# A written-out order searched anew, warm-up products in one run, and a last output tile stored in two halves

## The chip, the cores and the metric

The kernel runs on one core of one Trainium2 chip. A core has a matrix engine (TensorE, PE in the profile; its weight loads are listed apart as PEld), VectorE (DVE), ScalarE (ACT), GpSimd (POOL) and SyncE (SP), each with its own stream of instructions. POOL and SP issue DMA transfers. The metric is the device time of one execution in microseconds; the kernel before took 204.93 us (median of five runs, 204.13 to 205.15).

## The reference

Sparse attention is followed by a gated feed-forward block. With 4 batches, 8 heads, 768 positions, and heads of 64:

```python
k_chunks = k.reshape(B, H, nc, chunk, D)              # 24 chunks of 32 keys
ub = sum(maximum(q * k_min, q * k_max), axis=-1)      # a bound for each query and chunk
top_chunks = argsort(where(causal, ub, -1e9))[..., -6:]
attn = softmax(where(selected and causal, q @ k.T / 8, -1e9))
x = (attn @ v), heads side by side                    # [4, 768, 512]

h = maximum(x @ w_in, 0); u, v = h[..., :512], h[..., 512:]
v_n = (v - mean(v)) / sqrt(var(v) + 1e-6)
v_s = einsum('ts,bsd->btd', w_spatial, v_n) + b_spatial
out = (u * v_s) @ w_out                               # [4, 768, 512] float32
```

## The kernel before

Two heads of one batch make a pair; there are 16 pairs, four to a batch. A pair is worked on in steps, and each step is a small function with a name. The digits that follow a name are the pair and, after it, the head of the pair or a part; for the feed-forward steps they are the batch and the tile of 128 positions (0 to 5).

Attention steps of pair i:

- `lk`, `lq`, `lv`: loads of k, q and v, issued on POOL (for two pairs at once, except the first). `win`, `wsp`, `wout` and `lb` load the feed-forward weights there too.
- `kT`, `qT`: six and five transposes of 128x128 on TensorE. `kmax`, `kmin` (`k_bound`, L686) reduce the transposed keys over chunks on DVE, `kb` (L708) packs them, `rq` (L731, L733) takes the positive and negative part of q. `ub` is the product of both, the bound.
- `top` (L752) takes the eight largest bounds of each query, and `sel` (L778) writes the selection beside q. `aT` transposes q with its selection on TensorE, and `ac` (L800) copies that to SBUF on ACT or DVE. From pair 8 on, `aTd` (L803) does both as one DMA transpose from SP.
- `kh` (L574) sets up four pairs of score operands at the start from the constant `expand`; `kop` (L715, L717) copies the transposed keys into them. For pairs 0 and 1 ACT does it, for pairs 2 to 7 DVE, and from pair 8 on it is a DMA on SP, behind a copy `kc` (L703) of the keys from PSUM to SBUF.
- `sc` (L810) are the scores, six groups for a head, each in one of three PSUM banks; the selection is part of the product, since unselected chunks get a large negative term. `ex` (L819) is the exponential on ACT. `tri` (L825) clears the upper triangle on POOL, for batches 1 to 3.
- `av` (L836) is the product with v in three parts; there is one PSUM bank for it. `rc` and `nm` (L841, L846) divide by the sum on DVE. `x` brings the result into place, transposed: by TensorE and a DVE copy (`xp`, then L864) for pairs 0 to 3 and 15, by a DMA transpose from SP (L855) for the others.

Feed-forward steps of batch b, tile ti: `v` and `u` (products with `w_in`), `va` and `ua` (ACT), `bs` and `vs` (statistics on DVE), `rs` (ACT), `vn` (DVE), `s` (product with the transposed `w_spatial`), `gt` (L973, the gate on DVE, into one of three buffers), `gd` (L988, a DMA transpose of the gate from SP that frees this buffer), `o` (product with `w_out`), `oc` (L993, the copy from PSUM) and `os` (L997, the store on SP). The last two tiles take `gp`, transposes on TensorE, in place of the DMA. All feed-forward products have the line L930. They need all four pairs of their batch, so those of batch 0 start after `x3`, and those of a batch lie among the attention steps of the next.

The order of all this is not left to a scheduler. `ORDER` is one string with the names of all steps, and the kernel runs the functions in that order. Each engine's stream is the string with the other engines' steps left out, and each engine works strictly through its own. So a step that waits holds all steps behind it on its engine. The string was made by a planner in the same file (`Sim`, `build`): it has a cost for each step, limits on buffers, priorities by due time, and a list `flip` of steps that change between ACT and DVE. Of this, only the string, the engine of each step and a few sizes reach the chip.

At the start TensorE has 65 products of a zero tile, `dm0` to `dm64`, placed one by one among the first steps (L873). Nothing reads them.

Of the kernel before, what the change touches and what calls it, by code (L numbers as in the profile page):

```python
# [11 lines left out]
F32 = mybir.dt.float32  # L12
# [5 lines left out]
P = 128  # L18
# [148 lines left out]
def mmc(n): return max(n/2.4+2.5,25)/1000  # L167
DEF=dict(BEATS=12,pa=8,dve_a=(),qx=('ACT',),xp=4,mlp_first=13,mlp_mul=1.0,sc=3,tr=1,acc=1,ml=3,kbuf=3,qbuf=3,vbuf=3,ebuf=3,late=240,chunk=2,
  lk=40,lq=36,lv=18,kdma=99,kcp=2,kcdma=1,kc_act=(),shift=4,prep=0.0,tm=.8,lm=0.2,lm2=1.2,gp=(),head=1,lag=0.0,kp=27,ca=99,tree=0,svk=1.4,svw=1.15,flip=(),wide=0,pt=(),xd=(),dum=0,warm0=0.,qa_dve=(),ma_act=(),mkbuf=2)
PEL=0.2  # L170
def build(prm=None):
# [39 lines left out]
    for i in range(NPAIR):  # L211
# [34 lines left out]
        for hi in range(2):  # L246
            if (kd or kc) and p['kcdma']:
                op(f'kop{i}{hi}','SP',.5,deps=[kt],acq=[('kh',i)],uses=[kr],prio=pr((3 if hi==0 else 8)),dma=(.45,1.8))
            else:
                ke='ACT' if i<2 else 'DVE'  # L250
                kq=('acc',f'kb{i}') if kdup else kr
                op(f'kop{i}{hi}',ke,(.80 if ke=='ACT' else .46) if not tree else .30,.1,deps=[f'kTb{i}' if kdup else kt],acq=[('kh',i)],uses=[kq],prio=pr((3 if hi==0 else 8)))
# [69 lines left out]
    for b in range(B):  # L322
# [5 lines left out]
        o_=[group('o',b,ti,4,lambda c0,m,ti=ti: [f'gd{b}{ti}']+[f'wout{j}' for j in range(KO)],[('gT',f'{b}{ti}')]) for ti in range(NQT)]  # L328
# [32 lines left out]
    for b in range(B):  # L361
        for ti in range(NQT):
            q=s.ops[last('o',b,ti,4)].prio
            op(f'oc{b}{ti}','ACT',.465,.12,deps=[last('o',b,ti,4)],acq=[('o',f'{b}{ti}')],uses=[('ml',f'o{b}{ti}')],prio=q+.5)
            op(f'os{b}{ti}','SP',.5,deps=[f'oc{b}{ti}'],uses=[('o',f'{b}{ti}')],prio=q+.6,dma=(.7,1.6))
# [6 lines left out]
    for o in s.order:  # L372
        if o.name[:2]=='kh': o.alts=('DVE',.32)
        elif o.name[:3]=='kop' and o.eng=='ACT': o.alts=('DVE',.46)
        elif o.name=='rq01' and o.eng=='ACT': o.alts=('DVE',.40)
    for n in p['flip']:
        o=s.ops[n]; e,oc=o.alts; o.alts=(o.eng,o.occ); o.dur+=oc-o.occ; o.eng,o.occ=e,oc
    for k in range(p['dum']): op(f'dm{k}','PE',mmc(128),PEL,deps=['dz'],acq=[('sc','dm')] if k==0 else [],uses=[('sc','dm')],prio=-22+k*.15)
# [3 lines left out]
PLAN = {'late': 40, 'mlp_first': 8, 'qbuf': 4, 'kbuf': 4, 'vbuf': 4, 'dum': 65, 'warm0': 5.3, 'kcp': 8, 'flip': ['ac21', 'ac60', 'ac71', 'gd34', 'kc11', 'kc13', 'kc14', 'kc9', 'kh01', 'kh31', 'oc00', 'oc01', 'oc11', 'oc12', 'oc13', 'oc20', 'oc22', 'rq01'], 'gp': ((3, 4), (3, 5)), 'lm': 0.2, 'lm2': 1.2, 'tm': 0.8}  # L382

ORDER = """
dz id0 dm50 ring0 dm19 dm26 lk000 dm35 dm14 dm55 dm53 ring1 dm13 dm36 dm49 lk010 dm6 dm1 small dm46 dm60 ring2 lq010
ring3 lq000 id1 lk011 expand lk001 kT0 kh31 kh30 dm40 dm7 lq001 dm56 dm31 dm3 kmin0 dm62 kTb0 kh21 lq011 qT0 kmax0
kh20 dm27 dm10 dm15 qTb0 lk10 dm42 dm38 dm41 dm48 kh01 dm30 dm8 dm57 kop01 rq00 rq01 mlat kop00 kT1 lk11 kb0 dm54 dm11
dm43 dm44 dm24 kmax1 dm32 dm52 dm45 kh00 dm0 ub0 kTb1 lv0 top00 dm20 dm47 dm2 dm23 kh11 dm34 dm29 dm58 dm59 dm28 kmin1
dm4 dm5 dm25 dm63 dm61 dm39 dm64 dm22 qT1 kh10 mtri dm18 dm33 dm21 top01 dm51 dm37 dm17 dm16 selA0 kop10 lq10 sel0
aTA00 rq11 aTB0 dm12 rq10 dm9 kop11 lq11 acA00 aTA01 kb1 sc000 acB0 ub1 lk20 ex000 sc001 top10 sc002 ex001 sc004 acA01  # L390
kT2 lq20 ex002 top11 sc003 ex004 sel1 sc011 kop20 lk30 av000 ex003 sc005 kop21 ex011 sc013 kmax2 lq21 aT10 ex005 ex013
aT11 av001 kmin2 ac10 sc010 lk21 av002 ex010 sc100 rc00 kb2 qT2 nm00 ac11 win01 kT3 rq21 sc015 wsp3 sc012 ex100 rq20
qT3 wsp5 ex015 kmax3 sc102 ex012 sc014 lv1 ex102 sc112 kmin3 ub2 ex014 av010 sc101 ex112 top20 sc111 lk41 ex101 av011
rq31 sc103 av012 ex111 top21 sc104 lk31 rc01 ex103 sel2 sc113 kb3 ex104 rq30 sc105 aT20 nm01 ex113 sc115 lv2 ub3 kop31
ex105 av100 ac20 sc114 top30 av101 sc110 ex115 kop30 ex114 av102 lq30 sc203 top31 ex110 aT21 rc10 sel3 sc200 ex203
nm10 win30 sc202 qT4 ex200 ac21 kT4 ex202 win21 sc205 rq40 sc201 aT30 kmax4 ex205 ex201 sc215 sc212 av110 ex215 win00
kmin4 ex212 sc211 av111 sc210 ac30 av112 rq41 aT31 ex211 kb4 sc204 kop40 ub4 ex210 sc214 kop41 ex204 rc11 sc213 top40
kT5 ex214 lq31 nm11 sc300 ac31 xp0 top41 av200 kmin5 ex213 av201 sc301 ex300 av202 sel4 xp1 ex301 rc20 sc310 kmax5
sc311 wsp2 ex310 qT5 sc302 win31 nm20 ex311 sc303 rq51 ex302 av210 rq50 ex303 av211 kop51 sc305 aT40 ex305 kop50 av212
sc304 ac40 x0 sc313 kT6 win20 rc21 ex304 kb5 aT41 nm21 sc315 ex313 sc312 kmax6 ex315 sc404 ac41 win11 sc314 x1 xp2  # L400
ex312 win10 av300 kmin6 ub5 ex404 av301 sc401 lk61 ex314 top50 sc402 av302 ex401 sc403 top51 wsp0 rc30 ex403 sc400
sel5 nm30 ex402 aT50 kop61 av310 ac50 lk40 x2 av311 sc412 ex400 kop60 sc405 qT6 av312 kb6 ex412 wsp4 sc415 rq60 kT7
ex405 rc31 sc413 ex415 rq61 sc411 tri40 sc501 nm31 ex413 aT51 kop70 ex411 av400 lq41 xp3 kmax7 ac51 av401 sc410 av402
wsp1 ex501 x3 sc414 ub6 ex410 kmin7 sc502 v00.0 ex414 sc503 kop71 ex502 v00.2 tri41 rc40 sc504 top60 sc500 v02.0 ex504
nm40 wout1 v04.0 ex503 top61 lq40 av410 va00 sel6 v02.2 qT7 lk50 va02 v04.2 rq71 av411 ex500 sc514 rq70 av412 va04
sc511 bs00 aT60 ex514 v01.0 rc41 ac60 ex511 sc510 v03.0 vs00 kb7 ex510 bs02 sc600 ub7 ex600 v01.2 nm41 sc505 sc515
top70 v03.2 x4 ex505 va01 av500 top71 tri50 sc513 ex515 sc603 sel7 va03 wsT0 bs01 wout0 ex513 av501 aT61 wsc0 ex603
lv3 av502 sc602 wsT1 rc50 ac61 vs02 bs04 sc512 v05.0 ex602 wsc1 aT70 ex512 kT8 nm50 sc613 ac70 v05.2 kmin8 tri51 sc604
sc601 va05 av510 vs04 lk71 kc8 u01.0 ex604 kmax8 av511 ex601 qT8 lv4 u01.2 ex613 rq81 u00.0 ua01 vs01 rq80 sc611 sc605
sc610 bs03 ex611 lq50 u00.2 aT71 bs05 ua00 av512 wsT2 kb8 ex605 sc614 ac71 wsT3 tri60 ex614 wsc2 sc704 ub8 ex610 wsc3  # L410
wsT4 lk51 u02.0 vs05 ex704 rc51 vs03 top80 sc703 rs0 u02.2 lq51 nm51 ex703 sc612 wsT5 wsc4 ex612 av600 lb top81 sc701
ua02 sc700 vn04 u03.0 ex701 wsc5 sc702 av601 ex700 vn00 u04.0 ex702 vn01 u03.2 sel8 av602 sc615 u04.2 ua03 vn03 aTd8
kT9 ex615 vn02 ua04 sc705 s00.0 tri61 rc60 ex705 nm60 sc710 kc9 sc713 vn05 s00.2 tri70 kop80 ex710 av610 kmin9 x5
sc715 s00.4 ex713 wout2 u05.0 kmax9 lq60 av611 kop81 sc711 av612 qT9 kop90 ex711 rc61 s01.0 nm61 ex715 u05.2 rq91
av700 rq90 ua05 s01.2 kb9 sc714 gt00 av701 ub9 ex714 sc712 gd00 av702 top90 s02.0 rc70 s01.4 top91 sc803 sel9 kop91
s02.2 gt01 ex803 sc800 aTd9 kT10 ex712 nm70 s02.4 ex800 kmin10 sc805 qT10 tri71 ex805 sc801 gd01 sc810 kmax10 s03.0
ex801 wout3 av710 ex810 sc802 gt02 x6 sc804 av711 ex802 sc812 kc10 av712 ex804 s03.2 rc71 ex812 s04.0 kop100 nm71
tri80 sc814 kb10 gd02 sc815 rq101 kT11 ex815 s03.4 lq61 rq100 ex814 sc811 kmax11 av800 x7 ex811 s04.2 gt03 av801 sc813
av802 ub10 kop101 ex813 rc80 s05.0 kc11 sc900 tri81 sc905 sc901 nm80 s05.2 kop110 ex901 top100 lk60 s04.4 ex900 gd03
av810 gt04 s05.4 ex905 av811 sc911 kmin11 sc904 o00.0 ex911 av812 gt05 ex904 sc903 sc910 o00.2 top101 ex910 sc912  # L420
sel10 o02.0 ex903 oc00 aTd10 qT11 ex912 o01.0 rq111 sc902 rc81 o02.2 kb11 ex902 rq110 kop111 o01.2 nm81 oc02 ub11 gd04
tri90 v10.0 oc01 sc913 v11.0 lq70 x8 v10.2 v13.0 lv5 va10 sc914 v11.2 bs10 v13.2 va11 av900 v14.0 ex913 bs11 av901
va13 v12.0 top110 ex914 sc1002 av902 top111 v14.2 ex1002 bs13 o03.0 va14 v12.2 rc90 sel11 sc915 vs10 sc1000 nm90 va12
kT12 aTd11 o03.2 vs11 ex1000 kc12 v15.0 ex915 bs14 oc03 sc1003 tri91 sc1001 gd05 av910 kmin12 ex1001 v15.2 lq71 u10.0
ex1003 kmax12 kop120 sc1010 av911 qT12 lv6 ex1010 sc1004 vs13 bs12 u11.0 va15 u10.2 rq121 ex1004 av912 bs15 o04.0 ua10
u11.2 rc91 nm91 sc1005 kT13 ua11 kb12 sc1012 vs12 x9 vs14 o04.2 rq120 kc13 u12.0 vs15 oc04 ub12 kmax13 kop121 sc1013
# [33 lines left out]
def kernel(  # L460
# [407 lines left out]
    for n in range(prm["dum"]):  # L868
        @act(f"dm{n}")
        def warm(n=n):  # L870
            if "warm" not in tiles:
                tiles["warm"] = ps_sc.tile([P, 512], F32, tag="sc", name="warm")
# [170 lines left out]
```

## Time and profile before

| | |
|---|---|
| median of five runs | 204.93 us (204.13 to 205.15) |
| the profiled execution | 204.93 us, its span 203.2 us |
| granted TensorE clock, mean | 0.997 |
| busy: PE / DVE / ACT / POOL | 189.7 / 157.6 / 147.5 / 79.7 us |
| exponentials of 128x512 on ACT | 160, 88.1 us together, 611 ns each |
| chunk reductions on DVE (L686) | 32, 29.6 us, 949 ns each |
| DMA packets, bytes | 114617, 28.60 MB |
| v to SBUF, k to SBUF, issue to landing | 8.7 us, 6.5 us (medians) |
| output store of 256 KB, issue to landing | 2.8 us (median) |

A busy share is the time in which an engine has an instruction under way. Matmuls overlap one another, so a sum of their durations is more than the time that they take: the interval from one to the next is 0.216 us for 512 columns (ten in 2.16 us on the chain) and 0.056 for 128 columns once the clock is up (six in 0.34). The releaser in square brackets is what ended an engine's idle time. "PE", "DVE" and so on in the chain are the engines that the chain runs through; a DMA in it is time in which all waited for a landing.

### The profile page before, as it was taken

The page shows a single profiled execution, that of the slowest core. Times are in us where ns is not written, and L with a number is a line of the kernel's source. Part 1 is how long each engine was busy: PE and PEld are TensorE (multiplying, and loading weights), DVE is VectorE, ACT ScalarE, POOL GpSimd, SP SyncE. Part 2 cuts the span into 40 slices and gives each one's busy share as a digit, 9 for nine tenths or more (in the row PEclk, how much of TensorE's full clock was granted, in tenths as well). Part 3 has the DMA queues.
Part 4 walks back from the last instruction along what each step waited for, and adds up shares of the span by engine and source line. Part 5 has one row for each costly group of instructions (what it writes and reads, how often), then busy time and mean ns, then how long its engine had stood idle before and what let it go on. Part 6 is the DMA issues. An engine that isn't in the chain of part 4 may idle for free.

```text
span 203.2 us, 5218 instructions
## 1 busy us (share of the span) xinstructions
PE 189.7 (93%) x2012; PEld 119.4 (59%) x2012; DVE 157.6 (78%) x476; ACT 147.5 (73%) x292; POOL 79.7 (39%) x96
## 2 busy tenths in 40 slices
PE   3897999999999999997999999999999999999991
PEld 2886678767576756564555655565555565444440
DVE  6889899999899999886689968795886557366520
ACT  2878999899799994876398958688899471564051
POOL 7999874275637852260615321304303030000000
PEclk9999999999999999999999999999999999999998
DMA  5999999999999999999899997967983263150364
GB/s 38 110 122 155 156 163 138 167 184 154 120 106 106 138 122 174 168 159 136 150 147 154 160 244 197 106 165 174 175 196 117 57 163 79 53 208 0 77 207 183
DMA packets 114617, 28.60 MB, mean 141 GB/s; under 512 B 108704, under 2 KB 111008, under 8 KB 114592
## 3 DMA queue, kind: packets, MB, share of 16 engines
q0 software_dynamic: 76544, 12.20, 91.7%
q1 hardware_dynamic: 38048, 16.06, 37.6%
q8 instruction: 16, 0.26, 0.6%
q14 instruction: 9, 0.07, 0.2%
HBM read 24.38 MB, written 6.29 MB: 151 GB/s over the span
## 4 chain that ended last, share of the span: by engine, by line
PE 65%; DVE 17%; DMA 7%; POOL 4%; ACT 2%; issue 1%; SPq 1%; POOLq 0%; DVEq 0%
PE mlp L930 42%; PE sc L810 11%; PE acc L836 7%; DVE kmm L686 4%; DMA vt<-in_v_dram 4%; DMA gT<-g 4%; DVE kh L717 3%; DVE max L752 2%; DVE x L846 2%; POOL qs L604 2%; POOL k L604 2%; PE trq L722 1%; PE kTp L665 1%; PE ub L742 1%; DVE qs L778 1%
## 5 line engine op out<-in xcount | busy, mean ns | idle before, releaser
L819 ACT ACTIVATE e<-sc 128x512 f16<-128x512 f32 (+1 forms) x192 | 94.5, 558 | 20.9 <-PE sc L810 17.3
L810 PE MATMUL sc<-a,kh 128*128 128x512 f16 (+3 forms) x256 | 61.5, 305 | 0.8 <-DMA kh<-kT 0.5
L930 PE MATMUL mlp<-w_in_sb,xT 128*128 128x512 f16 x192 | 51.9, 379 | 0.0
L825 POOL TENSOR_SCALAR_AFFINE_SELECT e<-e 128x768 f16<-128x768 f16 x24 | 21.1, 884 | 75.9 <-ACT e L819 48.8
L836 PEld LDWEIGHTS <-e 128*128 128x128 f16 x672 | 31.5, 97 | 15.0 <-issue 2.0
L930 PE MATMUL mlp<-vn,wsT 128*128 128x512 f16 x144 | 38.8, 379 | 0.1
L836 PE MATMUL acc<-vt,e 128*128 128x65 f16 x672 | 35.8, 193 | 1.2 <-DMA vt<-in_v_dram 0.7
L686 DVE TENSOR_REDUCE kmm<-kTp 128x24 f16<-128x768 f16 x32 | 29.6, 949 | 2.1 <-ACT kT L703 1.0
L810 PEld LDWEIGHTS <-kh 128*128 128x128 f16 x256 | 22.8, 97 | 13.9 <-DMA kh<-kT 0.8
L973 DVE SCALAR_TENSOR_TENSOR g<-mlp,b_col,u 128x512 f16<-128x512 f32 x24 | 17.9, 749 | 13.1 <-PE mlp L930 10.8
L930 PE MATMUL mlp<-w_out_sb,gT 128*128 128x512 f16 x96 | 26.4, 379 | 0.1
L930 PEld LDWEIGHTS <-xT 128*128 128x128 f16 x192 | 16.9, 98 | 14.6
L952 DVE BATCH_NORM_STATS2 stats<-vraw 128x6 f32<-128x512 f32 x24 | 16.3, 682 | 7.0 <-ACT vraw L947 7.0
L993 ACT COPY o<-mlp 128x512 f32<-128x512 f32 x17 | 9.9, 589 | 14.2 <-PE mlp L930 14.2
L947 ACT ACTIVATE vraw<-mlp 128x512 f32<-128x512 f32 x24 | 14.5, 602 | 5.7 <-PE mlp L930 5.7
L930 PEld LDWEIGHTS <-wsT 128*128 128x128 f16 x144 | 12.5, 97 | 10.1 <-DVE vn L967 0.3
L846 DVE TENSOR_TENSOR x<-acc,rec 128x384 f16<-128x384 f32 x32 | 17.6, 551 | 0.5
L962 ACT ACTIVATE u<-mlp 128x512 f16<-128x512 f32 x24 | 14.1, 600 | 4.6 <-PE mlp L930 4.5
L752 DVE MAX8 max<-ub 128x8 f32<-128x8 f32 (+4 forms) x160 | 15.5, 166 | 1.1 <-PE ub L742 0.9
L595 POOL DMA_DIRECT2D qs<-in_q_dram x14 | 14.5, 1037 | 2.3 <-DMA vt<-in_v_dram 2.3
L589 POOL DMA_DIRECT2D k<-in_k_dram x14 | 14.6, 1041 | 0.7 <-DMA qs<-in_q_dram 0.7
L930 PEld LDWEIGHTS <-gT 128*128 128x128 f16 x96 | 8.8, 98 | 8.7 <-DMA gT<-g 0.8
(76 smaller groups left out, 233.0 us busy)
## 6 DMA issues: line engine op xcount, KB each, us to landing
out_dram<-o SPq DMA_DIRECT2D x24, 256.0 KB, 2.8
vt<-in_v_dram POOLq DMA_DIRECT2D x8, 384.0 KB, 8.7
k<-in_k_dram POOLq DMA_DIRECT2D x14, 192.0 KB, 6.5
qs<-in_q_dram POOLq DMA_DIRECT2D x14, 192.0 KB, 7.1
kh<-kT SPq DMA_DIRECT2D x16, 96.0 KB, 4.1
ws_raw<-in_moe_w_spatial_dram POOLq DMA_DIRECT2D x6, 192.0 KB, 7.3
w_in_sb<-in_moe_w_in_dram POOLq DMA_DIRECT2D x8, 128.0 KB, 8.3
w_out_sb<-in_moe_w_out_dram POOLq DMA_DIRECT2D x4, 128.0 KB, 3.7
```

The costliest lines, as they stand in the source:

```text
L589: nc.gpsimd.dma_start(out=k_tile(g)[:, :, :, hi, :].rearrange("p x t d -> p (x t) d"), in_=source(k, b, 2 * hp + 2 * hi, 2))
L595: nc.gpsimd.dma_start(out=t.rearrange("p x t d -> p (x t) d"), in_=source(q, b, 2 * hp + 2 * hi, 2))
L686: nc.vector.tensor_reduce(self.kmm[:, m, :], src.rearrange("d (c ch) -> d c ch", ch=CHUNK), axis=AX.X, op=op, negate=(m == 1))
L752: nc.vector.max(self.max8[:, qi - 1, hi, :], self.ub[:, c0:c0 + CPT * (qi + 1)])
L810: mm(sc[:, col:col + n], lhsT=self.kh[hi][:, t * P:(t + 1) * P], rhs=self.a[:, q0 // P:(q0 + n) // P, hi, :], start=True, stop=not diag)
L819: nc.scalar.activation(out=self.e[hi][:, g * 512:g * 512 + width], in_=self.sc[hi, g][:, 0:width], func=Act.Exp, scale=scale)
L825: nc.gpsimd.affine_select(out=blk, in_=blk, compare_op=Alu.is_ge, fill=0.0, base=0, channel_multiplier=-1, pattern=[[0, NQT], [1, P]])
L836: mm(self.av[hi][:, qi, :], lhsT=self.e[hi][:, c:c + P], rhs=self.v[hi][:, t, 0:D + 1], start=first and n == 0, stop=last and n == len(blo ...
L846: nc.vector.tensor_tensor(self.x16[:, :, hi, :], in0=self.av[hi][:, :, 0:D], in1=self.rec[hi].to_broadcast([P, NQT, D]), op=Alu.mult)
L930: mm(st[kind, ti], lhsT=lhsT, rhs=rhs, start=(j == 0), stop=(j == n - 1))
L952: nc.vector.bn_stats(st["stats", ti], st["vraw"][:, ti, :])
L973: nc.vector.scalar_tensor_tensor(g, in0=st["s", ti], scalar=b_col[:, ti:ti + 1], in1=st["u"][:, ti, :], op0=Alu.add, op1=Alu.mult)
```

## The change

Four things differ in the code.

- The 65 single products at the start become one step `dm` of 42 products in a row and 30 single ones, `dm0` to `dm29`.
- The last output tile (batch 3, tile 5) is worked in two halves of 256 columns: `o35.0` makes the left half, `oc35` copies it on ACT and `os35` stores it; `o35.2` makes the right half in a PSUM bank of its own, `od35` copies it on DVE and `ot35` stores it. Before, `o35.0` and `o35.2` were the two halves of the contraction over the full 512 columns.
- The planner has other costs for `kop` (0.57 for 0.46) and can choose their engine; options that the plan doesn't use were added (`pt`, `kdm`).
- With these, a new string `ORDER` and a new list `flip`. The loads, the DMA transposes and the k operand copies are the same transfers in number, size and queue, in another order; SP has one more store.

```diff
-PLAN = {..., 'dum': 65, 'warm0': 5.3, 'kcp': 8, 'flip': ['ac21', 'ac60', 'ac71', 'gd34', 'kc11', 'kc13', 'kc14', 'kc9', 'kh01', 'kh31', 'oc00', 'oc01', 'oc11', 'oc12', 'oc13', 'oc20', 'oc22', 'rq01'], ...}
+PLAN = {..., 'dum': 30, 'warm0': 5.3, 'kcp': 8, 'flip': ['ac60', 'ac71', 'gd34', 'kc11', 'kc13', 'kc14', 'kc8', 'kc9', 'kh11', 'kh20', 'kh21', 'oc00', 'oc10', 'oc11', 'oc13', 'oc14', 'oc21', 'rq01'], ..., 'dum0': 42, 'split': 1}
...
+    def warm(count):
+        if "warm" not in tiles:
+            tiles["warm"] = ps_sc.tile([P, 512], F32, tag="sc", name="warm")
+        for _ in range(count):
+            mm(tiles["warm"][:, 0:P], lhsT=idle_op, rhs=idle_op, start=True, stop=True)
+
+    acts["dm"] = lambda: warm(prm["dum0"])
     for n in range(prm["dum"]):
-        @act(f"dm{n}")
-        def warm(n=n):
...
+        acts[f"dm{n}"] = lambda: warm(1)
...
+        if prm["split"] and b == B - 1:
+            ti, half = NQT - 1, DM // 2
+
+            def o_half(n):
+                st["oh", n] = ps_ml.tile([P, 512], F32, tag="mlp", name="mlp")
+                for db in range(KO):
+                    mm(st["oh", n][:, 0:half], lhsT=st["gT", ti][:, db, :], rhs=w_out_sb[:, db, n * half:(n + 1) * half],
+                       start=(db == 0), stop=(db == KO - 1))
+
+            def o_half_copy(n):
+                if ("osb", ti) not in st:
+                    st["osb", ti] = ml.tile([P, DM], F32, tag="o", name="o", bufs=6)
+                copier("DVE" if n else "ACT")(st["osb", ti][:, n * half:(n + 1) * half], st["oh", n][:, 0:half])
+
+            def o_half_store(n):
+                nc.sync.dma_start(out=out[b, ti * P:(ti + 1) * P, n * half:(n + 1) * half],
+                                  in_=st["osb", ti][:, n * half:(n + 1) * half])
```

In the string, these places matter for what follows (each engine's part of it, in its order):

```
TensorE, first scores   before: sc000 ub1 sc001 sc002 sc004 kT2 sc003 sc011 av000 sc005 sc013 aT10 aT11 av001 sc010 av002
                        after:  sc000 ub1 sc001 sc002 kT2 sc004 sc003 sc011 sc005 av000 aT10 sc013 aT11 av001 sc010 av002
DVE, start              before: expand kh31 kmin0 kmax0 kh01 rq00 rq01 kb0 kmax1 top00 kmin1 top01 selA0 sel0
                        after:  expand kh21 kh11 kmax0 kmin0 rq00 kh20 rq01 kb0 kmin1 top00 kmax1 top01 selA0 sel0
DVE, near gt05          before: gt04 kmin11 gt05 top101 sel10
                        after:  gt04 top100 top101 kb11 sel10 gt05
SP, first transfers     before: x4 aTd8 kop80 x5 kop81 kop90 gd00 kop91 aTd9 gd01 x6 kop100 gd02 x7 kop101 kop110 gd03 aTd10
                        after:  x4 kop81 x5 kop80 aTd8 x6 gd00 aTd9 kop91 kop90 gd01 gd02 kop101 x7 gd03 kop110 kop100 gd04 aTd10
POOL, from lv0 on       before: lv0 mtri lq10 lq11 lk20 lq20 lk30 lq21 lk21 win01 wsp3 wsp5 lv1 lk41 lk31 lv2 lq30 ...
                        after:  lv0 lq10 mtri lq11 lk21 win01 lq21 lq20 lk20 lv1 lq31 lk31 wsp4 lk41 win00 lk30 lq30 ...
TensorE and SP, end     before: o35.0 o35.2, then oc35 (ACT), os35
                        after:  o35.0 (oc35 on ACT, os35) o35.2 (od35 on DVE, ot35)
```

## The prediction

> **What bounds the kernel now.** I read the page's forty slices and chain first, then busy time by stage, then the chain in order of time, then the matmuls before each gap.
>
> ```profile
> PE   3897999999999999997999999999999999999991
> DVE  6889899999899999886689968795886557366520
> PE 65%; DVE 17%; DMA 7%; POOL 4%; ACT 2%; issue 1%; SPq 1%; POOLq 0%; DVEq 0%
> ```
>
> TensorE is full nearly everywhere, but the slices don't say whether it is full of long or of short work. The stages do (columns: PE, weight loads, DVE, ACT, POOL busy):
>
> ```profile
> 14.90:20.80 5.90, 4.75 (x74) 3.57 (x72) 5.08 (x19) 4.82 (x10) 5.90 (x8) 1.00 2.48 154
> 20.80:51.20 30.40, 28.94 (x459) 22.39 (x459) 29.74 (x99) 29.35 (x61) 17.79 (x23) 1.00 2.22 159
> 51.20:80.00 28.80, 28.69 (x349) 19.10 (x348) 27.43 (x91) 25.07 (x52) 17.82 (x19) 1.00 1.58 125
> 80.00:97.00 17.00, 15.25 (x163) 9.06 (x161) 13.84 (x43) 11.09 (x23) 5.08 (x6) 1.00 1.44 159
> 97.00:198.74 101.74, 101.70 (x851) 55.53 (x849) 69.35 (x190) 67.14 (x138) 19.55 (x20) 1.00 0.88 141
> 198.74:203.20 4.46, 0.00 (x0) 0.00 (x0) 0.00 (x0) 0.58 (x1) 0.00 (x0) 0.85 0.48 181
> ```
>
> From 20.8 to 51.2 DVE idles 0.66 us and ACT 1.05: these two set the pace, and TensorE, without feed-forward products (they need all four pairs of batch 0), runs short work at their heels. From 51.2 (v00.0, the first feed-forward product) TensorE sets the pace, and all it loses stands between 80 and 97. Two landings pin the stage before, and three waits make the loss:
>
> ```profile
> 16.87 0.49 PE L665 MATMUL kTp<-identity,k 128*128 128x128 f16 x6 [0.40 <-DMA k<-in_k_dram]
> 18.60 0.43 PE L836 MATMUL acc<-vt,e 128*128 128x65 f16 x9 [0.70 <-DMA vt<-in_v_dram]
> ...
> 83.78 0.39 PE L810 MATMUL sc<-a,kh 128*128 128x512 f16 x1 [0.49 <-DMA kh<-kT]
> 94.81 0.75 DVE L973 SCALAR_TENSOR_TENSOR g<-mlp,b_col,u 128x512 f16<-128x512 f32 x1 [1.51 <-DMA gT<-g]
> 96.41 0.44 PE L722 MATMUL trq<-identity,qs 128*128 128x128 f16 x5 [1.05 <-DVE qs L778]
> ```
>
> The last two are one event: gt05 waits on DVE for the g buffer that gd02's transpose still reads (7.19 us in flight); sel10 stands behind it on DVE, and qT11 on TensorE behind that.
>
> **Clock at the start.** Products of 128 columns show the clock: six transposes took 0.80 us at 5.84 and 0.49 at 16.87; six weight loads take 0.58 us still at 9.84 and ten take 0.32 at 11.11, so the clock turns near 10.8. Before, 14 products ran from 1.06 to 2.74 and TensorE then waited 3.1 us for k. Now 42 (and 30 single ones later, 72 for 65) run unbroken: at 1.68/14 = 0.12 us each (0.10 by their weight loads) they reach to 5.3 or 6.1, and kT0 could start at 5.84. So the fast clock comes by 5 to 8 instead of 10.8. The Trainium skill, "TensorE: Matmul & The Clock Gate", Part 1, lets the clock double after a busy free-running window of about 3.4 us; the late turn here agrees, and by that rule 4.5 us unbroken may still miss a whole window. If all of it reached the end, four early groups of transposes (kT0, kTb0, the q pair, kT1) would give 0.3 us each, 1.2 in all: an estimate by that page.
>
> By the trace it doesn't reach the end. DVE gains 0.76 us of idle time at 10.72 (kmax1 waited for kT1) and pays 0.35 for one more expand copy (three, kh11, kh20, kh21, for two), so sc000 comes about 0.4 us earlier than 14.92. But kT2 can't start before 16.84, and it now stands before sc004 (which had its place ahead of it): ex004 slips from 16.98 to about 17.6. av000 can't start before vt lands at 18.56. SP does nothing yet, and POOL issues the same eleven loads up to lv0. On ACT, ex005 ends at 19.46 before; counted through (ex004 17.6, ex003, ex011, ex005, 0.53 each, the last 0.27) it ends at 19.5 now. DVE: kmin2, sel1, kmax2, kop20, kop21 from 17.37 are 0.91+0.41+0.91+0.56+0.56 = 3.35, so rc00 at 20.7 (20.77 before). **Head: 0**, bounds -0.4 (the lead kept) and +0.4 (ACT, idle 1 us before ex004, doesn't catch up).
>
> **DVE's stage, 20.8 to 51.2.** ac21 goes from DVE (0.55) to ACT (0.79), and kop70 (0.56) moves behind x3, whose end at 51.25 admits v00.0. DVE so has 1.1 us less before x3. ACT gets ac21 but ac51 is now behind x3: its sum is equal, and its 1.05 us of idle time caps the gain. Taken by either engine the products start 0 to 1.05 us earlier; I take 0.8, nearer DVE, because DVE's idle time is the smaller. Two groups, av402 and ub6, move behind v00.0: 6 x 0.03 + 11 x 0.025 = 0.45 us that TensorE must still do. **Net -0.35**, bounds -0.6 and +0.45. Loads moved: lv2 from 25th to 31st of POOL's issues, that is to about 37 us; landing at most 9.1 us later, 46, against its use at 49.3. lk30 from 16th to 25th, win30 from 27th to 35th; used at 40.7 and 51, landings near 37 and 49. Close, but covered.
>
> **The stretch 72 to 97.** I measure room in TensorE work (0.216 us for a 512-column product, 0.056 for 128, 0.03 for 65) between a transfer's place and its first user. kop81, the late one at 83.78 (6.4 us of room, 6.5 in flight), now has 20; kop80 7.8 for 5.5. sel10 stands before gt05, so gt05's wait no longer holds qT11, and gd02 has 7.5 us before gt05 instead of 6.3. That removes 0.49 + 1.05 = 1.54. New close places: kop90 has 5.2 us (11.7 before), and such copies took 2.7 to 6.5 here, so 0 to 1.3 late; gt03 comes 6.1 after gd00 (8.0) and gt04 6.5 after gd01 (7.7), with gate transposes of 4.6 to 7.2, so up to 1.1 and 0.7, with rq101, kmax11 and rq100 queued behind gt03 on DVE for qT's and ub's of pairs 10 and 11. lk51 now stands behind tri61 on POOL: 8.0 us of room for 4.7 to 6.7. I take 0.4 for kop90 and 0.4 for the gates, the middles of landings, since the medians there (5.5 and 5.3) sit near or under the rooms. **Net -0.7**, bounds -1.54 and +1.6 (1.3 + 1.1 + 0.7 = 3.1 against 1.54).
>
> Elsewhere after 97 the gaps between matmuls are only 0.43 us in all (155.6), rooms are much as they were, and copies that change engine (kc8 and oc01, oc12, oc20, oc22 to ACT, oc10, oc14, oc21 to DVE, 0.55 to 0.80 each) have over 32 us of idle time on either engine after 97 to lie in: 0.
>
> **The last tile.** o35 in two halves is eight products of 256 columns for four of 512: eight more issue costs of a few ns, 0.01. Nothing follows TensorE's last product but copy, store and landing. Before: copy 198.74 to 199.33, store 2.2 to 2.8. After: ACT copies the first half while TensorE runs the second, and DVE the second (0.42 for 512 columns of f16, 0.69 of f32; so about 0.35 to 0.4 for 256). That gains 0.2, but the second store queues on SP behind the first, 0.33 to 0.44 each. And the channel is full:
>
> ```profile
> GB/s 331 394 362 268 32 32 110 331 441 315 441 331 426 347 410 347 410 378 394 378 378 410 237 47 16 32 16 0 0 0 0 0 0 0 0 0 0 0 0 0
> ```
>
> In slices of 0.13 us from 198, the last three stores run at some 390 GB/s from 198.9 to 200.9 without a hole, and the bytes are the same. **-0.1**, bounds -0.35 (half the last store's 0.67) and +0.3 (one more issue on SP). The Trainium skill, "DMA: Bandwidth & Descriptors", Anatomy of one DMA, speaks against halves: its fit (for POOL's transfers, these are SP's) charges a fixed 2.0 us to each and 0.3 for 128 KB; by it the last half, issued when the whole tile was, would land 0.3 us sooner, an estimate. No row here shows a 128 KB store.
>
> **Sum.** 0 - 0.35 - 0.7 - 0.1 = -1.15. The profiled execution took 204.93 us (span 203.2 and 1.73 around it), which is the median of the five, so the forecast is 203.8, its own range 202.4 to 204.4.
>
> **Rivals.** (a) Hidden anyway: the lead ends at the two landings, ACT paces the middle (net +0.45), the late copies swap names (-0.5 for -0.7), 204.8. For it: every engine but TensorE loses its savings at some pin. Against: 1.54 us of old waits have a visible reason to go. (b) Slower, by SP alone: x6 to gd05 are 15 issues of 0.6 to 1.95 us, 17.4 to 18.2 us, written over 17.0 us of TensorE work, where before 16 took 18.4 of 20.6. If SP falls behind by 0.4 to 0.8 while transfers take 6.5 to 7.2, kop90 is 1.7 late, gt03 1.2, gt04 1.2: 4.1 against gains of 2.0, 207.0 in full, about 206 if half overlap. It decides when these waits pass 2.0 us together. Against: the SP queue enters the stretch with three of its transfers already done. (c) The clock isn't held: 30 products stand where 51 stood later, and if it falls back, the 4 us of work from 14.9 to 20 double inside 5.9 us: +2.1, with the rest 205.9. Against: gaps of 0.4 to 0.85 us at 16 to 19 don't slow it before.
>
> **Chances.** Forecast 0.53, (a) 0.18, (b) 0.22, (c) 0.07. 0.3% is 0.6 us, about what a measurement here can tell. The forecast is beyond that in nine of ten, (a) in one of six: faster 0.51, same 0.18, slower 0.31 (b, c and a little of a). Range 202.3 to 206.3: the forecast with its bounds, (a), (c) and the half of (b) with overlap.
>
> **What would show it.** Right: 128-column transposes at the fast rate by 8 us; av000 still at 18.6; v00.0 near 50.4; no wait of TensorE over 0.6 between 75 and 97; o35.2 ending 1 us earlier and the landing 3.9 us after it. Wrong: sc000 far from 14.5; kh<-kT or gT<-g releasing TensorE or DVE for over 1 us in the stretch; a new wait after 97; vt landing elsewhere than 18.56.

## The result, and the profile after

The changed kernel took 205.04 us (median of 53 executions, 203.57 to 207.87) where the kernel before, beside it, took 204.49 us (95 executions, 202.54 to 206.96). The ratio is 1.003, with a 95% interval of 1.0016 to 1.0043: slower by 0.3 to 0.9 us, where the prediction had 1.1 us of gain. Medians here and below are over all executions, while the ratios leave out those more than 1.5% above the fastest of their kernel, so a ratio can differ from that of two medians. The first profile of the changed kernel is of its longest execution (207.87 us), so the lines below are from a later one: 205.3 us, its span 203.5 us. The kernel before had 204.93 us and 203.2 us; the two profiled executions stand 0.4 us apart, the medians 0.55.

From the changed kernel's page, the busy tenths of the forty slices and the chain's shares by engine:

```profile
PE   7676799999999988999999999999999999999991
DVE  6996799999999999997579899595778437356520
PE 65%; DVE 19%; DMA 6%; POOL 6%; issue 1%; ACT 0%; POOLq 0%; ACTq 0%
```

TensorE has the nines of before, and eights in the slices between 71 and 81 us; the chain has two points more of DVE and two more of POOL. The stages (columns: PE, weight loads, DVE, ACT and POOL busy with instructions in brackets, clock, DMA share, GB/s):

```profile
14.90:20.80 5.90, 4.11 (x64) 3.05 (x61) 4.31 (x16) 4.30 (x9) 5.90 (x7) 1.00 2.51 154
20.80:51.20 30.40, 28.48 (x451) 22.20 (x449) 28.70 (x98) 29.37 (x62) 18.28 (x26) 1.00 2.02 157
51.20:80.00 28.80, 27.39 (x330) 17.92 (x329) 27.56 (x83) 24.51 (x53) 17.23 (x18) 1.00 1.87 128
80.00:97.00 17.00, 17.00 (x193) 10.50 (x193) 15.08 (x50) 12.04 (x25) 5.37 (x7) 1.00 1.51 153
97.00:199.33 102.33, 101.99 (x857) 55.83 (x855) 68.35 (x189) 68.22 (x140) 18.90 (x20) 1.00 0.84 142
199.33:203.50 4.17, 0.00 (x0) 0.00 (x0) 0.42 (x1) 0.08 (x1) 0.00 (x0) 0.95 0.52 189
```

The stretch from 80 to 97 us is now without a gap (17.00 of 17.00 busy, 15.25 before): what the prediction wanted there has happened. But the stage before it, 51.2 to 80, has lost: 27.39 busy and 330 products, where it had 28.69 and 349. The matmuls on which the prediction's steps stand, from the timeline of the changed kernel:

```profile
5.55 0.50 PE L673 MATMUL kTp<-identity,k 128*128 128x128 f16 x6
17.11 0.49 PE L673 MATMUL kTp<-identity,k 128*128 128x128 f16 x6 [1.42 <-DMA k<-in_k_dram]
19.07 0.43 PE L852 MATMUL acc<-vt,e 128*128 128x65 f16 x9 [0.23 <-DMA vt<-in_v_dram]
55.63 0.44 PE L738 MATMUL trq<-identity,qs 128*128 128x128 f16 x5 [0.29 <-DVE qs L794]
75.95 0.45 PE L852 MATMUL acc<-vt,e 128*128 128x65 f16 x9 [0.55 <-DVE x L862]
79.07 0.59 PE L950 MATMUL mlp<-vn,wsT 128*128 128x512 f16 x2 [0.57 <-DVE vn L987]
```

The first row is the early clock (0.50 us for six transposes, 0.80 before), the next two are the landings that pin the head. The last three are new. At `qT7` TensorE waits 0.29 us for DVE's `sel6`; then it waits 0.55 us for DVE's `nm` (which frees the bank of `av`) and 0.57 us for DVE's `vn`. All three stand, with the same lengths to 0.01 us, in the other profiles of the changed kernel too, and in none whose order in this stretch is that of before. Below, "both waits" are the last two.

What DVE and POOL do around them, from the timeline of the changed kernel (L987 is `vn`, L862 `nm`, L697 `kmin`; on POOL L841 is `tri`, L597 and L603 the loads `lk51`, `lk60`, `lq50`):

```profile
72.65 2.54 DVE L987 TENSOR_SCALAR vn<-vraw,mv,rstd 128x512 f16<-128x512 f32 x3
73.13 0.85 POOL L841 TENSOR_SCALAR_AFFINE_SELECT e<-e 128x768 f16<-128x768 f16 x1 [4.17 <-issue]
73.95 2.04 POOL L597 DMA_DIRECT2D k<-in_k_dram  x2
75.33 0.56 DVE L862 TENSOR_TENSOR x<-acc,rec 128x384 f16<-128x384 f32 x1
75.81 1.44 DVE L987 TENSOR_SCALAR vn<-vraw,mv,rstd 128x512 f16<-128x512 f32 x1
75.97 1.03 POOL L603 DMA_DIRECT2D qs<-in_q_dram  x1
77.16 0.94 DVE L697 TENSOR_REDUCE kmm<-kTp 128x24 f16<-128x768 f16 x1
78.03 0.99 DVE L987 TENSOR_SCALAR vn<-vraw,mv,rstd 128x512 f16<-128x512 f32 x2
```

The same six steps in the kernel before, with POOL's neighbours:

```profile
70.65 1.05 POOL L627 DMA_DIRECT2D b_col<-in_moe_b_spatial_dram  x1
70.77 0.53 DVE L967 TENSOR_SCALAR vn<-vraw,mv,rstd 128x512 f16<-128x512 f32 x1
71.68 0.99 DVE L967 TENSOR_SCALAR vn<-vraw,mv,rstd 128x512 f16<-128x512 f32 x2
72.91 0.99 DVE L967 TENSOR_SCALAR vn<-vraw,mv,rstd 128x512 f16<-128x512 f32 x2
74.10 1.86 POOL L825 TENSOR_SCALAR_AFFINE_SELECT e<-e 128x768 f16<-128x768 f16 x2 [2.40 <-ACT e L819]
74.51 0.73 DVE L967 TENSOR_SCALAR vn<-vraw,mv,rstd 128x512 f16<-128x512 f32 x1
```

Six `vn` of batch 0 are 3.24 us before (0.53 + 0.99 + 0.99 + 0.73) and 4.97 us after (2.54 + 1.44 + 0.99), for the same work. Where POOL is idle one takes 0.53 (two in a row 0.99, since they overlap a little); the one at 75.81, which starts in the last 0.2 us of one load's issue and lasts through the next, took 1.44. That was the first suspicion for the loss. DVE's other steps beside the same POOL work, `nm` with 0.56 us and `kmin` with 0.94, are as long as everywhere; they read PSUM, `vn` reads SBUF and writes SBUF.

### The profile page after: what moved, and what is told of

The parts are those of the page before. It is cut to its first block, busy times and chain, and to the rows that moved or that the text cites. A ratio compares the mean times of both kernels' runs of the same rounds, so it can differ in the third digit from the quotient of the medians.

```text
span 206.2 us, 5233 instructions
## 1 busy us (share of the span) xinstructions
PE 189.3 (92%) x2023; PEld 118.8 (58%) x2023; DVE 157.8 (77%) x475; ACT 146.9 (71%) x294; POOL 79.3 (38%) x96
## 4 chain that ended last, share of the span: by engine, by line
PE 59%; DVE 21%; DMA 10%; POOL 6%; issue 1%; ACT 1%; POOLq 0%; ACTq 0%
PE mlp L950 36%; PE sc L826 10%; PE acc L852 6%; DVE kmm L697 5%; DMA qs<-in_q_dram 4%; DVE vn L987 4%; DMA a<-qs 3%; DVE max L768 2%; DVE x L862 2%; DMA gT<-g 2%; DVE kh L733 2%; POOL qs L612 2%; PE trq L738 2%; POOL k L612 2%; PE kTp L673 1%
## 5 line engine op out<-in xcount | busy, mean ns | idle before, releaser
L950 PE MATMUL mlp<-w_in_sb,xT 128*128 128x512 f16 x192 | 52.7, 379 | 0.2 <-ACT u L982 0.2
L841 POOL TENSOR_SCALAR_AFFINE_SELECT e<-e 128x768 f16<-128x768 f16 x24 | 20.8, 866 | 79.1 <-ACT e L835 63.7
L697 DVE TENSOR_REDUCE kmm<-kTp 128x24 f16<-128x768 f16 x32 | 29.7, 948 | 2.6 <-PE kTp L673 2.1
L982 ACT ACTIVATE u<-mlp 128x512 f16<-128x512 f32 x24 | 14.6, 614 | 5.6 <-PE mlp L950 5.6
L862 DVE TENSOR_TENSOR x<-acc,rec 128x384 f16<-128x384 f32 x32 | 17.6, 552 | 0.4
L987 DVE TENSOR_SCALAR vn<-vraw,mv,rstd 128x512 f16<-128x512 f32 x24 | 14.7, 670 | 2.1 <-ACT rstd L1023 2.1
L597 POOL DMA_DIRECT2D k<-in_k_dram x14 | 14.5, 1034 | 3.2 <-DMA qs<-in_q_dram 1.2
L603 POOL DMA_DIRECT2D qs<-in_q_dram x14 | 14.4, 1033 | 0.0
```

The lines of the kernel that those rows point to most:

```text
L697: nc.vector.tensor_reduce(self.kmm[:, m, :], src, axis=AX.X, op=op, negate=(m == 1))
L841: nc.gpsimd.affine_select(out=blk, in_=blk, compare_op=Alu.is_ge, fill=0.0, base=0, channel_multiplier=-1, pattern=[[0, NQT], [1, P]])
L862: nc.vector.tensor_tensor(self.x16[:, :, hi, :], in0=self.av[hi][:, :, 0:D], in1=self.rec[hi].to_broadcast([P, NQT, D]), op=Alu.mult)
L950: mm(st[kind, ti], lhsT=lhsT, rhs=rhs, start=(j == 0), stop=(j == n - 1))
L982: nc.scalar.activation(u[:, ti, :], st["u", ti], func=Act.Relu)
L987: nc.vector.tensor_scalar(vn[:, ti, :], in0=st["vraw"][:, ti, :], scalar1=st["mv"][:, ti, 0:1], scalar2=st["rstd"][:, ti, :], op0=Alu.subt ...
```

## The experiments

**Where the loss is.** The order can be spliced: the names of one string up to a mark, then the names that are left, in the other string's order, each step on the engine that its own string has for it. `x3` is the last step of batch 0's attention (about 51 us), `v10.0` the first product of batch 1's feed-forward block (about 97 us). Four kernels ran on one chip: the changed one again, and three splices.

```diff
-ORDER = changed
+ORDER = changed up to x3, then before
...
-ORDER = changed
+ORDER = before up to x3, then changed
...
-ORDER = changed
+ORDER = before up to v10.0, then changed
```

> The changed kernel once more, for a second profile. Theory E (the loss lies before x3, since kT2, kmin2 and qT2 now stand where they hold more work back when a load lands late): ratio 1.002 to 1.005, v00.0 starting no earlier than 51.2. Theory M (the loss lies in the stretch 72 to 106, where a<-qs and the gates come late): the same ratio, v00.0 near 50.5 and over 2.5 us of gaps between matmuls from 72 to 106. My prediction had v00.0 at 50.4 and under 1.5 us of gaps in that stretch.

> The new order (and the 42 products in one run) up to the step x3, the old order for all that is left, old last tile. Theory E: as slow as the whole change, 1.002 to 1.005. Theory M: 0.995 to 1.000, since the late part is the old one and the start brings its 0.35 us. A loss in the last 100 us only would show here as 0.995 to 1.000 too.

> The old order and the old products up to x3, the new order for all that is left, with the last tile in two halves. Theory E: the loss is gone and the predicted gain of the stretch is there, 0.994 to 0.998. Theory M: the loss is here, 1.003 to 1.007.

> The old order up to v10.0 (about 97 us), the new order behind it, with the last tile in two halves. Theories E and M both: 0.998 to 1.001, since what they blame is the old order's here. Were it slower by 0.3% or more, the loss would lie behind 97 us, where I predicted nothing.

| | median, us | ratio to before | 95% interval |
|---|---|---|---|
| changed again | 204.41 | 1.0019 | 0.9992 to 1.0045 |
| changed up to x3, then before | 204.26 | 1.0008 | 0.9980 to 1.0037 |
| before up to x3, then changed | 205.68 | 1.0050 | 1.0023 to 1.0077 |
| before up to v10.0, then changed | 203.77 | 0.9992 | 0.9966 to 1.0019 |

The splice that takes the changed string from `x3` on is slower; the one that takes it only from `v10.0` on is not. So the loss comes from the changed string between 51 and 97 us, the stretch for which the prediction had the largest gain, and theory E (the loss lies in the head) falls. The two new waits are in the third profile (0.55 at 74.60, 0.56 at 77.72) and not in the second and fourth.

**The two other parts alone.** The kernel before with its first 14 warm-up products (`dm50` to `dm1`) replaced by one run of 42, and the kernel before with only the last tile in halves:

```diff
-dz id0 dm50 ring0 dm19 dm26 lk000 ...
+dz id0 dm ring0 lk000 ...
...
-... o35.0 oc34 os33 o35.2 os34 oc35 os35
+... o35.0 oc34 os33 oc35 o35.2 os34 os35 od35 ot35
```

> The kernel before with its first 14 warm-up products replaced by one run of 42, nothing else changed. By the prediction's step on the head (kT2 and av000 are pinned by landings, so that the early clock doesn't reach the end): fast transposes by 6 us, sc000 0.3 to 0.5 us earlier, ratio 0.998 to 1.001. Rival (the clock's gain of up to 1.2 us is kept): 0.994 to 0.997.

> The kernel before with only the last output tile worked, copied and stored in two halves. By the prediction's step (-0.1 us, bounds -0.35 and +0.3): ratio 0.998 to 1.0015, and the time from TensorE's last product to the span's end 4.1 to 4.5 us as before (4.5). Rival (a store of half the size lands in half the time): that time falls to 3.3 to 3.7 us and the ratio to 0.995 to 0.997.

The run of 42 alone measured 204.11 us, ratio 0.9996 (0.9967 to 1.0024), with the fast transposes at 6.19 us; the halves alone 204.68 us, ratio 1.0015 (0.9989 to 1.0041). Neither shows a gain or a loss. Rival readings, the clock's 1.2 us kept or a store that lands in half the time, would have shown at 0.994 to 0.997. The second falls: its interval begins at 0.9989, and from the last product to the end of the span it is 4.4 us, where 3.3 to 3.7 was expected of half the time. The first all but falls; its interval reaches down to 0.9967.

**The suspected cause taken away, with three loads.** In the changed kernel the three loads go ahead of `tri61` on POOL, so that they are issued before DVE comes to `vn`; and the same once more with `sc004` ahead of `kT2` and `kmin2` behind `sel1` in the head, as in the order before.

```diff
-lq51 tri61 lk51 lk60 lq50 tri70
+lq51 lk51 lk60 lq50 tri61 tri70
```

> The changed kernel with three loads (lk51, lk60, lq50) moved on POOL from behind tri61 to right behind lq51, so that POOL issues them some 5 us earlier, before DVE comes to batch 0's vn steps; all other engines' strings as changed. Theory P (the loss is DVE's: the vn steps, SBUF to SBUF, run beside POOL's issues at 1.0 to 1.4 us each instead of 0.5, and TensorE then waits for x and for vn, gaps of 0.7 and 0.7): vn of batch 0 at 0.5 to 0.75 us each, their sum some 1.5 to 2 us less, the two waits of TensorE near 76 and 79 us gone, ratio to the kernel before 0.996 to 0.999. Theory S (the loss is that transfers from SP come too late, aTd10 and the gates): vn may be shorter, but the ratio stays 1.001 to 1.005, and the wait of sc for a<-qs stays. Theory W (the new string simply puts more TensorE work before s00): ratio 1.001 to 1.005 and no wait of TensorE at 76 to 80 us that went.

> As the run with the three loads moved, and in the head sc004 put back ahead of kT2 and kmin2 behind sel1, as in the order before. If the place of kT2 holds TensorE where pair 2's keys land late (waits of 1.4 to 1.8 us at kT2 in two profiles of the changed kernel, 0.4 before), this gains 0.2 to 0.6 us more: ratio 0.994 to 0.998. If the landing of v sets the start of av000 in any order, it is equal to the run with the loads moved within 0.15%.

They measured 207.70 us, ratio 1.0169 (1.0119 to 1.0219), and 207.94 us, ratio 1.0113 (1.0075 to 1.0151): far slower, against every theory. The `vn` steps of the first of the two, and the only long wait of TensorE between 50 and 110 us:

```profile
71.11 2.06 DVE L987 TENSOR_SCALAR vn<-vraw,mv,rstd 128x512 f16<-128x512 f32 x3
73.79 0.54 DVE L987 TENSOR_SCALAR vn<-vraw,mv,rstd 128x512 f16<-128x512 f32 x1
75.11 0.99 DVE L987 TENSOR_SCALAR vn<-vraw,mv,rstd 128x512 f16<-128x512 f32 x2
```

```profile
83.31 0.38 PE L826 MATMUL sc<-a,kh 128*128 128x512 f16 x1 [3.55 <-DMA a<-qs]
```

So the local claim held: `vn` took 3.59 us instead of 4.97 (1.4 us less, a little under the 1.5 to 2 expected) and both new waits were gone. But another one came that theory P had not priced. `aTd8`, the first DMA transpose of q from SP, was issued at 73.3 us behind the loads. SP's record of its issue, in this kernel and in the changed one:

```profile
73.28 4.09 SPq L819 DMA_TRANSPOSE a<-qs  x1
74.39 1.83 SPq L819 DMA_TRANSPOSE a<-qs  x1
```

It landed 9.9 us after the issue (7.1 in the changed kernel, 4.4 in the kernel before). In the second kernel it was 10.2 us, with a wait of 3.65.

**The cause taken away without the pile.** Now `lq50` and `lk60` go the other way, behind `tri70`, since the first uses are `qT10` at 88.66 us and `kT12` at 104.62. In a second kernel `lk51` alone goes ahead; the third is the first with the head's order of before.

```diff
 two loads late
-lq51 tri61 lk51 lk60 lq50 tri70
+lq51 tri61 lk51 tri70 lq50 lk60
 two late, one early
-lq51 tri61 lk51 lk60 lq50 tri70
+lq51 lk51 tri61 tri70 lq50 lk60
```

> The changed kernel with lk60 and lq50 moved on POOL behind tri70, so that they are issued about 3 us later, when most of batch 0's vn steps are done; lk51 stays behind tri61, beside the vn steps. Theory P (the vn steps pay for POOL's issues beside them): one load is left beside them, vn of batch 0 some 1 us less in sum than in the changed kernel, the waits at 76 and 79 us shrink or go, and since no load comes earlier than in the changed kernel, aTd8 lands in time: ratio to the kernel before 0.996 to 1.000. If the loss of the changed kernel lies elsewhere: 1.001 to 1.004.

> As the run with two loads late, and lk51 moved ahead of tri61, behind lq51: no load is issued beside the vn steps before tri70, but one load more flies ahead of aTd8. Theory P alone: vn at 0.5 to 0.7 us each, ratio 0.995 to 0.999. If the pile of loads ahead of aTd8 is what cost 3.55 us with three loads moved (its landing took 9.9 us there), one load costs about a third of what three did: a wait of sc of pair 8 of 0 to 1.2 us, ratio 0.998 to 1.003.

> As the run with two loads late, and in the head sc004 ahead of kT2 and kmin2 behind sel1, as in the order before. If the landing of v alone sets av000: equal to the run with two loads late within 0.15%. If the place of kT2 costs in the executions where pair 2's keys land late: 0.1 to 0.3% less.

And the opposite: the kernel before, in which POOL is held back by a memset that nobody needs, so that its loads `lk51`, `lq51` and `lb` are issued beside `vn`.

```diff
+    pause = cp.tile([P, 1280], F16)
+    act("pz")(lambda: nc.gpsimd.memset(pause, 0.0))
...
-tri60 lk51 lq51 lb tri61
+tri60 pz lk51 lq51 lb tri61
```

> The kernel before with one added step on POOL, a memset of 128x1280 f16 ahead of lk51 that nobody waits for; it holds lk51, lq51 and lb back by 1.3 to 2.2 us, so that POOL issues them beside the vn steps of batch 0 (70.8 to 75.2 us), as in the changed kernel. Theory P: vn of batch 0 at up to 1.4 us, their sum 1 to 2 us more, s00 0.5 to 1.5 us later, ratio 1.002 to 1.007. If vn is slow in the changed kernel for another reason: vn as before (0.5 to 0.7), ratio 0.999 to 1.001.

| | vn of batch 0, us | new waits of TensorE, us | ratio to before | 95% interval |
|---|---|---|---|---|
| two loads late | 4.83 | 0.55, 0.56 | 1.0008 | 0.9980 to 1.0037 |
| two late, one early | 4.00 | none, 0.20 | 0.9976 | 0.9946 to 1.0005 |
| two late, old head | 4.84 | 0.55, 0.56 | 1.0016 | 0.9987 to 1.0046 |
| before, its loads on vn | 4.05 (3.24 without) | none | 1.0024 | 0.9998 to 1.0051 |

The one load `lk51` beside the first three `vn` is enough for both waits; with it away, the first goes and the second falls to 0.20 us. The timeline of "two late, one early":

```profile
67.79 1.03 POOL L597 DMA_DIRECT2D k<-in_k_dram  x1
71.48 2.07 DVE L987 TENSOR_SCALAR vn<-vraw,mv,rstd 128x512 f16<-128x512 f32 x3
71.96 0.86 POOL L841 TENSOR_SCALAR_AFFINE_SELECT e<-e 128x768 f16<-128x768 f16 x1 [3.14 <-PE sc L826]
74.16 0.54 DVE L987 TENSOR_SCALAR vn<-vraw,mv,rstd 128x512 f16<-128x512 f32 x1
75.38 1.27 POOL L603 DMA_DIRECT2D qs<-in_q_dram  x1
75.48 1.39 DVE L987 TENSOR_SCALAR vn<-vraw,mv,rstd 128x512 f16<-128x512 f32 x2
```

Alone, `vn` takes 0.54; three with a `tri` beside them take 2.07, so `tri` costs as well; two beside a load's issue 1.39 (0.99 alone), and that issue 1.27 instead of 1.03. The head's order makes no difference clear of the noise: 1.0016 for 1.0008 here, 1.0113 for 1.0169 with the three loads ahead.

The old order with its loads on `vn`, same view:

```profile
69.50 1.16 POOL L571 MEMSET pause<- 128x1280 f16 x1
70.61 1.03 POOL L591 DMA_DIRECT2D k<-in_k_dram  x1
71.63 1.17 POOL L597 DMA_DIRECT2D qs<-in_q_dram  x1
71.64 0.53 DVE L969 TENSOR_SCALAR vn<-vraw,mv,rstd 128x512 f16<-128x512 f32 x1
72.56 1.32 DVE L969 TENSOR_SCALAR vn<-vraw,mv,rstd 128x512 f16<-128x512 f32 x2
72.79 0.84 POOL L629 DMA_DIRECT2D b_col<-in_moe_b_spatial_dram  x1
```

`vn` grew there too, by 0.8 us in sum, so the effect isn't tied to the changed string. It is less than the 1 to 2 us expected, and only 0.3 of it stands in the row of 1.32; most of the rest is the last `vn`, beside a `tri` that moved too. The expectation that `s00` comes later missed: from `v00.0` to `s00.0` it is 22.85 us, as before (22.86). The old order had room for it. The 1.0024 can't be told from no change, and isn't explained by this.

**The mended order beside the changed one, and the pile by one load more.** All four on one chip: the changed kernel, "two late, one early" again, the same with the last tile of before, and a kernel with `lk51` and `lq50` ahead and `lk60` behind `tri70`.

```diff
 two early, one late
-lq51 tri61 lk51 lk60 lq50 tri70
+lq51 lk51 lq50 tri61 tri70 lk60
```

> The changed kernel once more, on the chip on which the next three run. As measured so far: ratio to the kernel before 1.001 to 1.004.

> The run with two loads late and one early once more (0.9976, interval 0.9946 to 1.0005). Theory P (the vn steps slowed by POOL's issues are the whole of the loss): 0.3 to 0.6% under the changed kernel, ratio to the kernel before 0.996 to 0.999. If the first measurement was chance and part of the loss lies elsewhere: equal to the changed kernel within 0.15%.

> The run with two loads late and one early, with the last output tile as in the order before (one copy, one store of 256 KB). If halves gain nothing (halves alone measured 1.0015, interval 0.9989 to 1.0041): equal to the run with halves within 0.15%, ratio 0.996 to 0.999. If halves gain the 0.1 us of the prediction, or its bound of 0.35: 0.05 to 0.17% above it.

> The changed kernel with lk51 and lq50 moved ahead, behind lq51, and lk60 behind tri70: one load more ahead of aTd8 than in the run that did well, one less than in the run where aTd8 landed 9.9 us after its issue. If the landing grows with each load ahead of it: 6 to 8 us, no wait or one of up to 1.5 us at sc of pair 8, ratio 0.997 to 1.006. If it was lk60 alone (its place in the queue) that held it: 4.4 to 5.5 us, ratio 0.996 to 0.999.

Then the third of them once more, on another chip:

> The run with two loads late, one early and the old last tile once more (0.9968, interval 0.9932 to 1.0004). If it is faster than the kernel before: 0.995 to 0.999 again, and with the first measurement the two intervals together leave out 1. If the mend only brings back what the change lost: 0.999 to 1.002.

| | median, us | ratio to before | 95% interval |
|---|---|---|---|
| changed | 205.70 | 1.0076 | 1.0041 to 1.0112 |
| two late, one early | 204.03 | 0.9986 | 0.9952 to 1.0020 |
| the same, old last tile | 204.02 | 0.9968 | 0.9932 to 1.0004 |
| two early, one late | 207.84 | 1.0130 | 1.0095 to 1.0166 |
| old last tile, once more | 203.50 | 0.9956 | 0.9923 to 0.9988 |

Three moved loads, and nothing else, take the changed kernel from 1.0076 to 0.9986 with intervals that don't meet: the place of these issues is what made the change slower, and the waits that go with it are those behind `vn`. TensorE's records show the size: from `v00.0` to the first product with `w_out` it is 42.5 us in each of the three profiles of the changed kernel, and 41.4 to 41.7 in the four of the mended order. That the waits behind `vn` are all of the difference isn't shown: "two loads late" keeps both, needs 42.3 us for the same way, and measured 1.0008, on another chip and with an interval that overlaps both others. With the last tile of before, the mended order is faster than the kernel before: in its second measurement the interval leaves out 1, in the first it reaches to 1.0004. Whether the halves cost something is open, since 0.9986 and 0.9968 have intervals that overlap widely.

Two loads ahead of `aTd8` are as bad as they looked. It landed 4.6 to 4.9 us after its issue with `lk51` ahead, 7.9 with two loads, 9.9 and 10.2 with three; SP was busy with its issue for 2.4 to 2.6, 4.0 and 4.0 to 4.1 us. So it grows with the loads ahead, and is not `lk60` alone. Loads close to it count too: 7.1 and 7.7 in the changed kernel, which issues `lk51` and `lk60` within 0.6 us of it, and 6.2 and 6.4 with two loads late. Why two loads cost 1.3% isn't shown by that kernel's profile, which is of its shortest execution (205.09 us) and has no wait over 0.82 us.

## Why the prediction was wrong, step by step

**The step that failed** is the stretch from 72 to 97, -0.7 in the sum. Of POOL the prediction said: "lk51 now stands behind tri61 on POOL: 8.0 us of room for 4.7 to 6.7". That was right for the landing; no step waits for these loads. But the load was priced only by when it lands, and not by what its issue does to the engine beside it. `vn` was taken at no cost of its own, and it is the step that paid: 1.7 us of DVE time (4.97 for 3.24), of which 1.4 goes with the three issues (3.59 without them) and the rest with `tri`. Of it 0.55 + 0.57 = 1.12 us reached TensorE; with the mended order 0.20 is left.

The Trainium skill, "SBUF — State Buffer", Who interferes with whom, says that VectorE's two-port modes, which a `tensor_scalar` can enter, share a pair of ports with GpSimd under an exclusive lock, and that whichever starts first keeps it for the whole instruction. The rows here agree in direction: `vn`, a `tensor_scalar` from SBUF to SBUF, at 0.53 alone and 1.44 beside loads' issues of 1.03 us each, while `nm` and `kmin`, which read PSUM, stayed at 0.56 and 0.94. Who comes first seems to count too: not every `vn` beside an issue pays. One that starts within 0.12 us of the issue's start takes its 0.53 (70.77 in the kernel before, 71.64 in the old order with its loads on `vn`), and there the issue is the longer one: 1.05 us for `lb`, 0.84 in the other kernel, and 1.17 for `lq51`, 1.03 elsewhere. A `vn` that an issue holds ends 0.22 to 0.25 us behind the issue's end (77.25 for 77.00, 76.87 for 76.65 and 73.88 for 73.63 in the rows above). That the lock is the mechanism is argued from this, not shown; the runs show that moving the issues moves the cost.

**In the same step, the removed waits were taken too large.** The 1.54 us (0.49 for `kop81`, 1.05 behind `gt05`) were read from one execution. In six profiles whose order in this stretch is that of before, the first wait is 0.49 and 0.53 in two and absent in four, the second 1.05, 1.04, 1.00 and 0.32 in four and absent in two: (1.02 + 3.41)/6 = 0.74 us on average. The changed order did remove both. Take eight profiles with the changed order here: those with two or three loads moved ahead are left out, and so are two executions of over 207 us. The price put on `kop90` (0.4) was nothing to TensorE in all eight, and that on the gates (0.4) came in one of them, with 0.40 us: 0.05 on average. A wait that the prediction hadn't named, of `sc` for a DMA transpose of q, came with 1.06, 0.79 and 0.27 us in three of the eight: 0.27 on average. So the step, -1.54 + 0.4 + 0.4, becomes -0.74 + 1.12 + 0.05 + 0.27 = +0.7.

**Head, 0:** right in its number. `sc000` came at 14.44 (14.5 said), the fast transposes at 5.55. `av000` starts at 18.41 us on average in six profiles with the old head and at 18.40 in eleven with the new one (two of these with `sc004` and `kmin2` put back); it moves by 1.8 us from one execution to the next. In all six it waits for v's landing, in the eleven only in five; the other six come at much the same time, 17.72 to 18.99. `kT2` waited 1.42 us for its keys, and `sc004` behind it; putting it back changed nothing clear of the noise.

**DVE's stage, -0.35:** taken too good; this is the second step that failed. It was -0.8 for an earlier `v00.0` and +0.45 for `av402` and `ub6`, which move behind it. From `av000` to `v00.0` it is 32.66 us on average in the six, 32.12 in the eleven: -0.54 where -0.8 was said. The 0.45 still has to be done. And `kop70`, moved behind `x3`, comes back there: it stands on DVE ahead of `sel6`, for which `qT7` waits the 0.29 us of the rows above. In the splice that has `kop70` before `x3` and the changed order behind it, this wait is absent. So the net is -0.54 + 0.45 + 0.29 = +0.2. The splice that has only the head and this stage measured 1.0008 (0.998 to 1.0037), -0.4 to +0.8 us: no gain is seen there either.

**The last tile, -0.1:** inside its bounds. The halves alone are 1.0015 (0.9989 to 1.0041). From TensorE's last product to the end of the span it is 4.1 to 4.4 us with halves, and 4.1 to 4.5 with the whole tile. The GB/s of forty slices after the last product, in the changed kernel:

```profile
GB/s 0 138 314 393 393 373 373 393 354 413 393 354 373 413 324 334 334 363 324 334 363 334 148 10 0 0 0 0 0 0 0 0 0 0 0 0 0 0 0 0
```

The last bytes move 2.5 us after the last product (slice 24 of 40 in 4.17 us), and 1.7 us more pass in which nothing moves. In that last part a smaller store has nothing to shorten.

**The rivals.** "Hidden anyway" (204.8) came nearest in its number, with the wrong reason: the gains were not hidden but paid back. "The clock not held" falls: it was 1.00 in every stage up to the last product. "SP falls behind" holds in part: the waits for `aTd` are SP's, but in the changed kernel they are small beside the cost on DVE. The side on which the time fell was decided by none of them. With 0, +0.2, +0.7 and about 0 for the last tile the new sum is +0.9 us, the upper end of the +0.3 to +0.9 measured. Another count takes all of TensorE's gaps of 0.1 us and over from `v00.0` to its last product: 1.98 us on average in five profiles with the changed order and both waits (1.69 to 2.33), 1.36 in six with the order of before in this stretch (0.75 to 2.05). With -0.54 and +0.45 that is +0.5. So the waits and the moved work carry the loss, as closely as single profiles can tell.

## What to carry to other kernels

When a DMA issue is moved along GpSimd's stream, price it twice: by the room until its landing is needed, and by what VectorE does while it is issued; a step from SBUF to SBUF went from 0.5 to 1.4 us here. A load issued earlier isn't free either: two or three of them ahead of a transposing DMA held it for 8 to 10 us, where it took 4.4 in the kernel before. And a wait seen in one profile is worth its mean over several executions; to find where a long order loses, splice the two orders at marks and time the splices.

## What the runs showed of the hardware that was not expected

TensorE's clock fell after a single wait. In the kernel with three loads moved, TensorE idled 3.55 us and started again at 83.31; these are its windows then (clock third from the right):

```profile
83.00:84.00 1.00, 0.69 (x9) 0.48 (x10) 0.09 (x1) 0.00 (x0) 0.00 (x0) 1.00 1.32 257
84.00:85.00 1.00, 1.00 (x6) 0.46 (x5) 0.97 (x3) 0.20 (x1) 0.00 (x0) 0.60 1.23 260
85.00:86.00 1.00, 1.00 (x9) 0.72 (x8) 0.55 (x2) 1.00 (x3) 0.00 (x0) 0.50 1.24 323
86.00:87.00 1.00, 1.00 (x12) 0.73 (x11) 0.36 (x1) 0.37 (x1) 0.00 (x0) 0.50 0.59 126
87.00:88.00 1.00, 1.00 (x7) 0.40 (x5) 0.10 (x1) 0.00 (x0) 0.00 (x0) 0.69 0.22 45
```

At half speed from about 84.2 to 87.6 us (0.8 + 1 + 1 + 0.6 = 3.4 us), which makes the 3.55 us dearer: from `s00` to the first product with `w_out` it was 21.17 us, and 19.63 in the twin with the other head, which waited 3.65 us and kept its clock at 1.00. The same wait so costs 1.5 us more in one execution than in another. A third wait of this length, 3.19 us for a DMA transpose of q when "two late, one early" was run again, left the clock at 1.00 too. The Trainium skill, "TensorE: Matmul & The Clock Gate", Part 1, has the clock watched in free-running windows of 3.4 us; the length of the slow stretch agrees, and that two of three such waits were spared would fit windows that don't start with the wait.
